# Who loads wk and who loads wv: swapping two weight loads between SyncE's and ScalarE's queues at the start of an attention and MLP kernel

## The chip, the cores and the metric

The kernel runs on one core of one Trainium2 chip. The metric is the device time of one execution in microseconds (us), taken as the median of several runs. The changed kernel is timed beside the kernel before on the same chip.

## What is computed

The reference mixes two branches of the same x (2048 tokens of 512 features, bf16) by a gate of one number per token. Branch A is attention with 32 heads of 16 features in four segments of 512 tokens: causal softmax attention inside a segment, plus a read of a memory M, z that earlier segments have filled. Branch B is a gated MLP of width 1792.

```python
q, k, v = x @ wq, x @ wk, x @ wv              # split into 32 heads, 4 segments
for s in range(4):
    p = softmax(qs @ ks.T * scale + mask)
    a_dot = p @ vs
    a_mem = (phi(qs) @ M) / (phi(qs) @ z + 1e-6)
    o = sigmoid(beta) * a_mem + (1 - sigmoid(beta)) * a_dot
    M, z = M + phi(ks).T @ vs, z + phi(ks).sum()
a = concat(o) @ wo
b = (relu(x @ W_gate) * (x @ W_up)) @ W_down
g = sigmoid((x * gate_w).sum(-1))
out = g * a + (1 - g) * b
```

## The kernel before

The program is recorded as a list of operations with what they read and write, and a planner in the file (class Sched) then writes one instruction stream for each engine. It places operations by priority queues with assumed durations and landing times of loads, and inserts the semaphore waits. LAND0 (L36) holds such assumed landing times for the first loads. They change no instruction by themselves; they can only change the order that the planner writes, and which of 16 DMA semaphores a load gets. Once the order is written, each engine runs its own in that order.

The work goes by segments of 512 tokens. For each, TensorE does the projections of Q and K (L797, for the first segment's Q L802) and of V (L795), the attention products (L924, L980), the MLP's two input products (L1054) and its output product (L1093). ScalarE does the exponentials, VectorE most copies out of PSUM, GpSimd the causal masks, and SyncE (SP) issues nearly all DMAs.

The change is in the start, where nothing is in SBUF yet. All matmuls of the projections need x with the features on the partitions, xT (four tiles of 128 features by 512 tokens). For the first segment it comes in two ways:

- Tokens 0 to 255 are loaded as they lie (into hT, L628, from SP). TensorE transposes them with eight matmuls against an identity (L710), two for each of the four feature tiles, into four PSUM banks. Four copies (L717) bring them to xT. The list at L701 says which engine does each copy: VectorE, ScalarE, VectorE, VectorE.
- Tokens 256 to 383 and 384 to 511 come by two transposing DMAs from SP (L632, ldxb2 and ldxb3), straight into xT.

The loop at L629 issues the weights. Each of wq, wk and wv is four loads of 128 KB, one for each 128 input features. wq goes to SP (its last quarter to ScalarE's queue), wk to ScalarE's queue, wv to SP. The two transposing DMAs are put in SP's list just ahead of wv. SP then issues the halves of W_gate and W_up, and small tensors.

ScalarE's queue is a list of its own: lact holds three tiny loads, the quarter of wq and the warming of the exponential's table, then comes its copy of xT, and behind it the four loads taken out as `wks` (L651, L721):

```python
    wks = lact[1:5]
    lact = [lact[5], lact[0]] + lact[6:] + [tab]
    ...
    sc.queue(0, lact + xcs["act"] + wks)
```

TensorE's order in the first segment (L830 to L833) is: warming matmuls, the eight transposes, Q for tokens 0 to 255 (sixteen matmuls, feature tile by feature tile, the four column blocks in turn), Q for tokens 256 to 383 (sixteen), Q for 384 to 511 (sixteen), the first two column blocks of K (feature tile by feature tile, two matmuls for each, so that each quarter of wk is waited for in turn), the other two of K, and then V, which takes wv's four quarters. Attention and MLP follow.

Of the kernel before, what the change touches and what calls it, by code (L numbers as in the profile page):

```python
# [32 lines left out]
H1_T = 14000.0  # L33
LX = 300.0
DCOST = {"ldwg0_0": 1000.0, "ldbraw": 1800.0, "ldgwb": 1300.0, "ldx1_0": 1500.0, "vsh0": 1100.0, "vsh1": 1100.0, "vsh2": 1100.0, "vsh3": 1100.0}
LAND0 = {"ldhT0": 2850.0, "ldxb2": 3700.0, "ldxb3": 3500.0, "ldwq0": 2950.0, "ldwq1": 3050.0, "ldwq2": 3100.0, "ldwq3": 3700.0, "ldwk0": 2800.0, "ldwk1": 2900.0, "ldwk2": 3000.0, "ldwk3": 3000.0}  # L36
NBLK = 36
QTN, EKN, HTN, OTN, XR = 8, 4, 19, 8, 3
SBX = 0
# [89 lines left out]
class Sched:  # L129
# [241 lines left out]
    def place(self, op, e, start):  # L371
# [30 lines left out]
        if op.dma:  # L402
# [7 lines left out]
            issued = start + occ  # L410
            op.end = max(self.dma_busy + self.dcost(op) if op.nbytes > 4096 and op.name not in LAND0 else 0.0, start + self.landing(op, start) + (0.0 if op.name in LAND0 else LX))
            self.dma_busy = max(self.dma_busy, op.end) if op.nbytes > 4096 else self.dma_busy
# [21 lines left out]
    def landing(self, op, start):  # L434
        kind = op.name[:2] if op.name[:3] != "ldx" or op.name[:4] == "ldxr" else "tx"
        if op.name == "ldwd":
            return 10300.0
        if op.name in LAND0:
            return LAND0[op.name]
        if kind == "ld":  # L440
# [120 lines left out]
def build_kernel(nc, A_x, A_wq, A_wk, A_wv, A_wo, A_beta, W_g, W_u, W_d, gate_w, out):  # L561
    _, S, D = A_x.shape
    F = W_g.shape[1]
    assert D == 512 and S % 512 == 0 and F % 128 == 0
    NSEG, KT, NF, NT = S // 512, D // 128, F // 128, S // 128
    EPS, SCALE = 1e-6, 16 ** -0.5
    sc = Sched(seeds=(339564, 801711, 0, 805551, 301395, 836631, 634535, 0, 524381, 836447, 792364, 880187, 245227, 322538, 537582, 772576, 302341, 920238, 2826, 48651, 0, 987459, 126639, 0, 821755, 0, 0, 0, 0, 0, 349994, 0,))
    T = {}
    with contextlib.ExitStack() as stack:
        for name, shape, dt in plan(S, D, F):  # L570
            T[name] = stack.enter_context(nc.sbuf_tensor(name, shape, dt))
        PS = stack.enter_context(nc.psum_tensor("ps", [128, 8, 512], F32))
        for st in sc.streams:
            sc.sem[st] = stack.enter_context(nc.semaphore(f"s_{st}"))
        program(sc, nc, T, PS, A_x, A_wq, A_wk, A_wv, A_wo, A_beta, W_g, W_u, W_d, gate_w, out, NSEG, KT, NF, NT, EPS, SCALE)
        with nc.Block() as block:
            sc.emit(block)
    return sc


def program(sc, nc, T, PS, A_x, A_wq, A_wk, A_wv, A_wo, A_beta, W_g, W_u, W_d, gate_w, out, NSEG, KT, NF, NT, EPS, SCALE):
    V = type("V", (), T)
# [3 lines left out]
    def op(eng, fn, occ, **k):  # L586
        return sc.add(Op([(eng, fn, occ)], **k))

    def pe(fn, occ, **k):
        k.setdefault("lat", PE_LAT)  # L590
        if k.get("role") == "w":
            k["reads"] = list(k.get("reads", ())) + [f"init{i}" for i in range(4)]
        return op("pe", fn, occ, **k)
# [13 lines left out]
    def dma(eng, fn, nbytes, occ=500.0, **k):  # L607
        return op(eng, fn, occ, dma=True, nbytes=nbytes, **k)

    def A(ep):  # L610
        return PS[:, ep.bank, :] if ep.nb == 1 else PS[:, ep.bank:ep.bank + 2, :]
# [6 lines left out]
    def load(eng, names, dst, src, nbytes, occ=474.0):  # L618
        (lact if eng == "act" else lsp).append(dma(eng, lambda e, dst=dst, src=src: e.dma_start(dst, src), nbytes, occ=occ, writes=names, name="ld" + names[0]))  # L619
# [6 lines left out]
            load_xt("sp", c, kt)  # L626
    x0 = A_x[0, 0:512, :].rearrange("(h p i) d -> h p i d", h=2, i=2)
    load("sp", ["hT0", "hT1"], V.hT[:, 0:2, :], x0[0], 1 << 18)  # L628
    for eng, nm, w, src in (("sp", "wq", V.wq, A_wq), ("act", "wk", V.wk, A_wk), ("sp", "wv", V.wv, A_wv)):  # L629
        if nm == "wv":  # L630
            for i in (2, 3):
                lsp.append(dma("sp", lambda e, i=i: e.dma_start_transpose(V.xT[:, :, 128 * i:128 * i + 128], A_x[0, 128 * i:128 * i + 128, :]), 1 << 17, occ=1250.0, writes=[f"xT0_{i + 2}"], name=f"ldxb{i}"))  # L632
        for kt in range(KT):
            load("act" if (nm, kt) == ("wq", 3) else eng, [f"{nm}{kt}"], w[:, kt, :], src[kt * 128:(kt + 1) * 128, :], 1 << 17)
# [58 lines left out]
    def warm(m, n, k, b):  # L693
        def fn(e):
            for i in range(m):
                ins = e.matmul(PL[:, b, 0:n], lhsT=nc.const_aps.tensor(1.0, [128, 128], BF16), rhs=nc.const_aps.tensor(1.0, [128, n], BF16), start=True, stop=True)
            return ins
        return pe(fn, m * n * (0.834 if k == 0 else 0.5), writes=[f"bankL{b}"], name=f"warm{k}")

    xps, xcs = [warm(5, 512, 0, 3), warm(6, 128, 0, 3)], {"dve": [], "act": []}  # L700
    for h, kt, bank, eng in ((0, 0, 0, "dve"), (0, 1, 1, "act"), (0, 2, 2, "dve"), (0, 3, 3, "dve")):  # L701
        ep = Epoch("att") if bank is None else None
        bk = [] if bank is None else [f"bankL{bank}"]

        def B(ep=ep, bank=bank):
            return A(ep) if bank is None else PL[:, bank, :]

        def fx(e, h=h, kt=kt, B=B):
            for i in range(2):
                ins = e.matmul(B()[:, 128 * i:128 * i + 128], lhsT=V.hT[:, 2 * h + i, kt * 128:(kt + 1) * 128], rhs=V.ident[:], start=True, stop=True)  # L710
            return ins
        xps.append(pe(fx, 205, reads=[f"hT{2 * h}", "ident"], writes=bk, name=f"xt{4 * h + kt}", ep=ep, role=ep and "w"))
        dst = V.xT[:, kt, h * 256:(h + 1) * 256].rearrange("q (t i) -> q t i", i=2)

        def cpy(e, d=dst, B=B, eng=eng):
            x = B()[:, 0:256].rearrange("q (i t) -> q t i", i=2)
            return e.tensor_copy(d, x) if eng == "dve" else e.activation(d, x, ACT.Copy)  # L717
        xcs[eng].append(op(eng, cpy, 430 if eng == "dve" else 390, reads=bk, writes=[f"xT0_{kt + 4 * h}"], name=f"xc{4 * h + kt}", ep=ep, role=ep and "r"))
# [495 lines left out]
```

## Time and profile before

| | |
|---|---|
| time, median of 3 runs | 264.72 us (264.42 to 264.75) |
| the profiled execution, its own time | 264.86 us |
| its span in the profile | 263.1 us |
| TensorE (PE) busy | 254.3 us, 97% of the span |
| VectorE (DVE), ScalarE (ACT), GpSimd (POOL) busy | 182.4, 181.1, 128.6 us |
| DMA queue of the loads issued by SP (q1) | 18.80 MB, 30.9% of 16 engines over the span |
| DMA queue of the loads issued by ScalarE (q10) | 0.66 MB, 1.2% |

The profile is of one execution. A row of its timeline gives start and duration in us, the engine (PE matmuls, PEld weight loads of TensorE, SPq and ACTq the DMA-issuing instructions of SP and ScalarE), the line of the kernel, and what is written from what; x4 stands for four instructions in a row. The duration of a DMA-issuing instruction is only the issuing; "DMA to landing" is from the start of the issue to the data's being there. In brackets stands how long the engine was idle before, and what released it. The time outside the span, 264.86 less 263.1, is 1.76 us.

### The profile page before, as it was taken

Reading aid. Unit: us, or ns where it says so; the run is one execution under the profiler, and the core shown is the slowest. Engines: PE = TensorE matmul, PEld = TensorE weight load, DVE = VectorE, ACT = ScalarE, POOL = GpSimd, SP = SyncE. Lnnn points to the kernel's source line nnn. Section 1 sums busy time; section 2 is a strip of 40 time slices with the busy share of each in tenths; the row PEclk is TensorE's granted clock in tenths of the full one; section 3 lists DMA queues with packets and bytes.
Section 4 is the critical chain, followed back from the end, with each engine's and each line's share of the span. In section 5 each row is a group of like instructions: output and inputs, shape, how many; then the busy total and the mean of one; then the engine's idle time right before and its main releaser. Section 6 shows DMA issues by size and latency. Waiting matters only on the chain.

```text
span 263.1 us, 6472 instructions
## 1 busy us (share of the span) xinstructions
PE 254.3 (97%) x2643; PEld 114.9 (44%) x2677; DVE 182.4 (69%) x359; ACT 181.1 (69%) x153; POOL 128.6 (49%) x295
## 2 busy tenths in 40 slices
PE   8799999999999999999999999999999999999996
PEld 4533444443434544344344544444444434344444
DVE  4489888887787586887888588757575627478600
ACT  2377689879889678796777688677777566756021
POOL 3016533576558356665746386646364344444100
PEclk9999999999999999999999999999999999999999
DMA  7999653392515143202040430000031500000011
GB/s 176 314 349 207 152 51 41 90 342 54 82 40 108 27 79 80 75 8 43 22 107 20 62 102 2 22 4 20 13 81 36 59 21 22 22 0 2 0 42 40
DMA packets 35869, 19.87 MB, mean 76 GB/s; under 512 B 25088, under 2 KB 35200, under 8 KB 35840
## 3 DMA queue, kind: packets, MB, share of 16 engines
q1 hardware_dynamic: 35024, 18.80, 30.9%
q10 hardware_dynamic: 816, 0.66, 1.2%
q8 instruction: 21, 0.34, 0.5%
q14 instruction: 8, 0.07, 0.1%
HBM read 10.14 MB, written 2.11 MB: 47 GB/s over the span
## 4 chain that ended last, share of the span: by engine, by line
PE 92%; DVE 2%; DMA 2%; issue 2%; SPq 1%; POOL 0%
PE ps L1054 37%; PE ps L1093 18%; PE ps L924 9%; PE ps L797 8%; PE ps L980 7%; PE ps L1086 5%; PE ps L795 5%; DMA xT<-in_A_x_dram 2%; PE ps L867 1%; PE ps L847 1%; SPq L619 1%; SPq L632 0%; PE ps L802 0%; POOL E L946 0%; DVE kp L820 0%
## 5 line engine op out<-in xcount | busy, mean ns | idle before, releaser
L946 POOL TENSOR_SCALAR_AFFINE_SELECT E<-E 64x256 bf16<-64x256 bf16 (+1 forms) x256 | 108.8, 435 | 112.7 <-ACT E L940 84.5
L940 ACT ACTIVATE E<-ps 128x2048 bf16<-128x2048 f32 x72 | 135.0, 1876 | 40.9 <-PE ps L924 40.4
L1054 PE MATMUL ps<-xT,wg 128*128 128x512 bf16 x217 | 58.6, 380 | 0.8 <-issue 0.5
L1054 PE MATMUL ps<-xT,wu 128*128 128x512 bf16 x216 | 57.8, 380 | 1.0 <-issue 0.8
L1093 PE MATMUL ps<-wd,hT 128*128 128x512 bf16 (+2 forms) x227 | 52.1, 366 | 1.5 <-issue 1.4
L1065 DVE TENSOR_TENSOR hT<-ps,rl 128x512 bf16<-128x512 f32 x56 | 38.2, 683 | 14.4 <-PE ps L1054 13.0
L1054 PEld LDWEIGHTS ps<-xT,wu 128*128 128x128 bf16 x224 | 20.6, 98 | 25.6 <-issue 2.6
L1093 PEld LDWEIGHTS ps<-wd,hT 128*128 128x128 bf16 x238 | 21.2, 98 | 23.6 <-issue 2.6
L990 DVE STREAM_TRANSPOSE Tn<-ps 128x512 f32<-128x512 f32 x32 | 21.2, 695 | 14.6 <-PE ps L980 14.6
L1054 PEld LDWEIGHTS ps<-xT,wg 128*128 128x128 bf16 x224 | 19.9, 98 | 25.6 <-issue 4.7
L1063 DVE TENSOR_SCALAR rl<-ps 128x512 bf16<-128x512 f32 x35 | 24.1, 687 | 8.5 <-PE ps L1054 8.2
L924 PE MATMUL ps<-qT,kp 32*128 32x192 bf16 (+7 forms) x512 | 28.6, 287 | 0.0
L924 PEld LDWEIGHTS ps<-qT,kp 32*128 32x128 bf16 x512 | 8.2, 92 | 26.2 <-issue 11.4
L980 PE MATMUL ps<-E,vaug 64*17 64x128 bf16 (+7 forms) x512 | 18.7, 283 | 0.0
L980 PE MATMUL ps<-E,vsh 64*17 64x128 bf16 (+7 forms) x512 | 18.3, 283 | 0.0
L1103 ACT ACTIVATE osb<-ps,omg 128x512 bf16<-128x512 f32 (+1 forms) x9 | 6.1, 675 | 17.7 <-PE ps L1086 14.0
L1062 ACT ACTIVATE rl<-ps 128x512 bf16<-128x512 f32 x21 | 12.5, 596 | 7.2 <-PE ps L1054 7.1
L1086 PE MATMUL ps<-wo,oT 128*128 128x512 bf16 (+2 forms) x66 | 16.0, 366 | 0.1
L797 PE MATMUL ps<-xT,wk 128*128 128x512 bf16 x62 | 15.8, 379 | 0.2 <-issue 0.2
L1102 DVE TENSOR_SCALAR osb<-ps,omg 128x512 bf16<-128x512 f32 (+1 forms) x8 | 5.3, 665 | 15.2 <-PE ps L1086 10.4
L795 PE MATMUL ps<-wv,xT 128*128 128x512 bf16 x62 | 15.4, 380 | 0.2 <-issue 0.2
L980 PEld LDWEIGHTS ps<-E,vaug 64*17 64x17 bf16 x512 | 11.6, 86 | 8.3 <-issue 3.0
(70 smaller groups left out, 232.7 us busy)
## 6 DMA issues: line engine op xcount, KB each, us to landing
vsh<-vaug SPq DMA_DIRECT2D x8, 272.0 KB, 3.6
osb<-in_A_x_dram SPq DMA_DIRECT2D x16, 128.0 KB, 2.3
out_dram<-osb SPq DMA_DIRECT2D x15, 128.0 KB, 1.7
wg<-in_B_W_gate_dram SPq DMA_DIRECT2D x8, 224.0 KB, 5.4
wu<-in_B_W_up_dram SPq DMA_DIRECT2D x8, 224.0 KB, 6.4
wd<-in_B_W_down_dram SPq DMA_DIRECT2D x1, 1792.0 KB, 8.7
wk<-in_A_wk_dram ACTq DMA_DIRECT2D x4, 128.0 KB, 4.3
wv<-in_A_wv_dram SPq DMA_DIRECT2D x4, 128.0 KB, 4.2
```

Source lines behind the costliest of these rows:

```text
L795: ins = e.matmul(A(ep)[:, :], lhsT=V.xT[:, kt, tok + col * 128:tok + (col + 1) * 128], rhs=w[:, kt, :], start=(kt == 0), stop=(kt == KT - 1))
L797: ins = e.matmul(A(ep)[:, :], lhsT=w[:, kt, col * 128:(col + 1) * 128], rhs=V.xT[:, kt, tok:tok + 512], start=(kt == 0), stop=(kt == KT - 1))
L924: ins = q.matmul(dst, lhsT=V.kp[r, kslot(s, G), c, :], rhs=V.qT[r, qslot(s, G), q0:q0 + w], start=True, stop=True, tile_position=(32 * jj, ...
L940: acts.append(act(lambda a: a.activation(V.E[:, base * 512:base * 512 + min(2048, 4 * W)], PF[:, 0:min(2048, 4 * W)], ACT.Exp, scale=SCALE ...
L946: pools.append(pool(lambda g, ap=ap, lim=lim, pat=pat: g.affine_select(out=ap, in_=ap, compare_op=ALU.is_ge, fill=0.0, base=lim, pattern=[ ...
L980: ins = q.matmul(A(eps[p])[32 * jj:32 * jj + 17, 64 * (c + u):64 * (c + u + n)], lhsT=v[:, 8 * G + 2 * jj + p, :], rhs=V.E[r, f:f + 64 * n ...
L990: ds.append(dve(lambda e, p=p, ep=eps[p]: e.transpose(V.Tn[:, 2 * (G % (TNN // 2)) + p, :], A(ep)[:, :]), t_dve(512), writes=[f"Tn{2 * (G ...
L1054: ins = e.matmul(A(ep)[:, :], lhsT=w[:, kt, f * 128:(f + 1) * 128], rhs=V.xT[:, kt, c % XR * 512:(c % XR + 1) * 512], start=(kt == 0), sto ...
L1063: ("dve", lambda e, ep=eg, r=r: e.tensor_scalar(V.rl[:, r, :], A(ep)[:, :], 0.0, None, ALU.max), t_dve(512))],
L1065: evs.append(dve(lambda e, ep=eu, r=r, hs=hs: e.tensor_tensor(V.hT[:, hs, :], A(ep)[:, :], V.rl[:, r, :], ALU.mult), t_dve(512), reads=[f" ...
L1086: ins = e.matmul(A(ep)[:, 0:c1 - c0], lhsT=V.oT[:, ot[G], i * 128:(i + 1) * 128], rhs=V.wo[:, G, c0:c1], start=st_ and G == 0, stop=sp_ an ...
L1093: ins = e.matmul(A(ep)[:, 0:c1 - c0], lhsT=V.hT[:, slots[f], i * 128:(i + 1) * 128], rhs=V.wd[:, f, c0:c1], start=st_ and f == f0, stop=sp ...
```

## The change

wk's four loads go to SP, behind the second transposing DMA, where wv's stood. wv's four loads go to ScalarE's queue, where wk's stood (the list `wks` now holds wv's). The fourth copy of xT (feature tile 3) goes from VectorE to ScalarE, so that ScalarE's queue has two copies ahead of those loads. The planner's assumed landing times of wk become 2850 for each quarter. In the order that the planner writes, each engine's other instructions stand as before; some of the loads use another of the 16 DMA semaphores.

```diff
-LAND0 = {..., "ldwk0": 2800.0, "ldwk1": 2900.0, "ldwk2": 3000.0, "ldwk3": 3000.0}
+LAND0 = {..., "ldwk0": 2850.0, "ldwk1": 2850.0, "ldwk2": 2850.0, "ldwk3": 2850.0}
...
-    for eng, nm, w, src in (("sp", "wq", V.wq, A_wq), ("act", "wk", V.wk, A_wk), ("sp", "wv", V.wv, A_wv)):
-        if nm == "wv":
+    for eng, nm, w, src in (("sp", "wq", V.wq, A_wq), ("sp", "wk", V.wk, A_wk), ("act", "wv", V.wv, A_wv)):
+        if nm == "wk":
             for i in (2, 3):
                 lsp.append(dma("sp", lambda e, i=i: e.dma_start_transpose(...), ..., name=f"ldxb{i}"))
         for kt in range(KT):
             load("act" if (nm, kt) == ("wq", 3) else eng, [f"{nm}{kt}"], w[:, kt, :], src[kt * 128:(kt + 1) * 128, :], 1 << 17)
...
-    for h, kt, bank, eng in ((0, 0, 0, "dve"), (0, 1, 1, "act"), (0, 2, 2, "dve"), (0, 3, 3, "dve")):
+    for h, kt, bank, eng in ((0, 0, 0, "dve"), (0, 1, 1, "act"), (0, 2, 2, "dve"), (0, 3, 3, "act")):
```

More of the change, by code (lines that the diff above doesn't have):

```diff
@@ L35 @@
 DCOST = {"ldwg0_0": 1000.0, "ldbraw": 1800.0, "ldgwb": 1300.0, "ldx1_0": 1500.0, "vsh0": 1100.0, "vsh1": 1100.0, "vsh2": 1100.0, "vsh3": 1100.0}
-LAND0 = {"ldhT0": 2850.0, "ldxb2": 3700.0, "ldxb3": 3500.0, "ldwq0": 2950.0, "ldwq1": 3050.0, "ldwq2": 3100.0, "ldwq3": 3700.0, "ldwk0": 2800.0, "ldwk1": 2900.0, "ldwk2": 3000.0, "ldwk3": 3000.0}
+LAND0 = {"ldhT0": 2850.0, "ldxb2": 3700.0, "ldxb3": 3500.0, "ldwq0": 2950.0, "ldwq1": 3050.0, "ldwq2": 3100.0, "ldwq3": 3700.0, "ldwk0": 2850.0, "ldwk1": 2850.0, "ldwk2": 2850.0, "ldwk3": 2850.0}
 NBLK = 36
```

## The prediction

> **What bounds the kernel now.** I read the page first, then the waits of TensorE, then the chain of work that ended last, cut to the first 30 us, because the change touches only instructions that run before 10 us.
>
> ```profile
> span 263.1 us, 6472 instructions
> PE 254.3 (97%) x2643; PEld 114.9 (44%) x2677; DVE 182.4 (69%) x359; ACT 181.1 (69%) x153; POOL 128.6 (49%) x295
> ...
> PE ps L802 <- DMA xT<-in_A_x_dram: 1.3, 1, 1.3
> ...
> 4.02 4.87 DMA xT<-in_A_x_dram
> 8.88 0.05 issue
> 8.93 1.07 PE ps L802 x16
> 10.00 0.05 issue
> 10.05 3.40 PE ps L797 x15
> ```
>
> The first two rows say that TensorE is busy for 97% of the span, so what moves its first matmuls moves the end, nearly one for one. The waits (total, times, longest) show one DMA wait on TensorE in the whole run: 1.3 us of the Q projection (L802) for x. The chain says which: the second transposing DMA of x, in flight from 4.02 to 8.88 us. Sixteen matmuls of Q follow it, then the K projection (L797) from 10.05. All that the change can do to the time it does by moving the 8.88, or by making K wait where it doesn't wait today. 1.3 us, 0.5% of the span, is the largest gain from the first.
>
> **The change, part by part.** These are the rows of the timeline at the place (start, duration, engine and line), and below them the time from issue to landing of the four wk loads and the two transposing loads, and of the first and the last wv load alone.
>
> ```profile
> 3.65 0.63 PE L710 MATMUL ps<-ident,hT 128*128 128x128 bf16 x8
> 3.98 1.09 DVE L717 CAST xT<-ps 128x256 bf16<-128x256 f32 x3 [0.83 <-PE ps L710]
> 4.09 0.38 ACT L717 ACTIVATE xT<-ps 128x256 bf16<-128x256 f32 x1
> 4.10 1.95 ACTq L619 DMA_DIRECT2D wk<-in_A_wk_dram  x4
> 4.46 3.16 PE L802 MATMUL ps<-xT,wq 128*128 128x256 bf16 x32 [0.18 <-DVE xT L717]
> 5.32 2.00 SPq L619 DMA_DIRECT2D wv<-in_A_wv_dram  x4
> 9.87 1.09 ACT L808 ACTIVATE qT<-ps 128x512 bf16<-128x512 f32 x2 [5.39 <-DMA wk<-in_A_wk_dram]
> 11.17 0.43 SPq L619 DMA_DIRECT2D gwb<-in_gate_w_dram  x1
> 13.29 1.89 PE L795 MATMUL ps<-wv,xT 128*128 128x512 bf16 x8
> ...
> DMA to landing us min/median/max: 3.5/4.3/4.5
> DMA to landing us min/median/max: 3.5/4.2/4.9
> L619 SPq DMA_DIRECT2D wv<-in_A_wv_dram x1: 582/582/582, 5.3 to 5.3; - x1
> DMA to landing us min/median/max: 4.4/4.4/4.4
> L619 SPq DMA_DIRECT2D wv<-in_A_wv_dram x1: 430/430/430, 6.9 to 6.9; - x1
> DMA to landing us min/median/max: 4.1/4.1/4.1
> ```
>
> The copy first. VectorE loses one of three copies (1.09/3 = 0.36 us) and ScalarE gains one of 0.38. TensorE's transposes end at 3.65 + 0.63 = 4.28, so the second copy starts when the first ends, 4.09 + 0.38 = 4.47, and ends at 4.85, before VectorE's third did (3.98 + 1.09 = 5.07). TensorE needs it for the last quarter of the first Q matmuls. They end at 4.46 + 3.16 = 7.62, 1.3 us ahead of the x it then waits for. So the copy is worth nothing in itself; without that cover it would be 0.2 us, 5.07 less 4.85. ScalarE has nothing else to do until 9.87.
>
> What the copy does is delay the loads behind it. Today the first wk load is issued at 4.10, just after the copy starts. Behind a second copy I put wv's first issue at 4.4 to 4.5 and its last end near 6.4. That wv is late harms nobody: with the 4.5 us of the slowest wk load, the last piece lands before 11 and is first used at 13.29.
>
> Now wk on SP. It takes the four places of wv, so SP issues as much as before and nothing behind it moves, but for its waits: each load waits for the semaphore it reuses, and gwb, at 11.17, now follows the first wk load, which lands by about 9.7. At wv's durations wk lands at 5.3 + 4.4 = 9.7 to 6.9 + 4.1 = 11.0. K's first eight matmuls go through wk's four pieces, two matmuls each; by the chain's 3.40 us for 16 (one record is missing) a pair takes 0.43, so the pieces are wanted at 10.05, 10.48, 10.90 and 11.33. The margins are 0.35 and 0.33 at the two ends: wk is in time today, but no longer by much, and TensorE can't come forward by more than about 0.3 unless wk does.
>
> So two terms are left: when the second transposing DMA lands, and whether wk, now behind it in the same queue, slips. The shares of the two queues (q1 is SP's, q10 is ScalarE's: packets, MB, share of 16 engines), in five windows, 4.4 to 5.1, 5.1 to 5.7, 5.7 to 6.3, 6.3 to 7.5 and 7.9 to 9.3 us:
>
> ```profile
> q1 hardware_dynamic: 471, 0.16, 102.1%
> ...
> q10 hardware_dynamic: 84, 0.08, 56.8%
> q1 hardware_dynamic: 145, 0.03, 30.2%
> ...
> q1 hardware_dynamic: 332, 0.08, 90.7%
> q10 hardware_dynamic: 45, 0.03, 57.3%
> ...
> q10 hardware_dynamic: 102, 0.10, 72.2%
> q1 hardware_dynamic: 154, 0.04, 20.3%
> ...
> DMA packets 521, 0.45 MB, mean 318 GB/s; under 512 B 86, under 2 KB 521, under 8 KB 521
> ```
>
> First window: SP's queue alone, the first transposing load goes through. Second: a gap in SP's queue, in which ScalarE's takes 0.08 MB of wk. Third: the second transposing load starts, briskly. Fourth: wk's packets hold 72% of the engines for 0.10 MB in 1.2 us, and the tail of the transposing load creeps. The landings say the same: 3.5 us for the first, 4.9 for the second. That tail is the 1.3 us that TensorE waits.
>
> After the change wv stands where wk stood, 0.3 to 0.4 us later. The same competitor is there in the fourth window. What moved in the gap (84 packets) can now stand beside the transposing load instead of ahead of it: 0.08 MB at the 318 GB/s of the last window is 0.25 us. So the landing moves by between -1.4 (as quick as the first, 3.5 for 4.9) and about +0.3 (all of the lost gap); I take +0.1, nearest to the second, since the competitor stays. For wk: behind the transposing load it shared the engines with two leftover ACT loads today and shares with about three afterwards, the same 0.25 us at most on the last pieces, against a margin of 0.33. I take +0.1 for what of it shows on TensorE. Everything behind is in the same order on each engine, and no DMA wait of TensorE follows that could swallow or add to it.
>
> The Trainium skill's page "DMA: Bandwidth & Descriptors", section "Issuing engines are not separate DMA queues", says that loads from several engines run on the same DMA engines and interleave, so that spreading them saves only issue time. By that rule alone the swap of engines would be worth 0, and the sum 264.7; the trace agrees in so far as both queues share the engines in the windows above.
>
> The sum: 0 for the copy, +0.1 for the landing, +0.1 for wk, so +0.2. The profiled execution took 264.86 us (span 263.1 and 1.76 around it), and 265.06 is what it would become; the median of the runs, 264.72, is 0.14 lower, and becomes 264.9.
>
> **The rivals.** *The transposing load escapes (faster).* The later start of the ACT loads takes them out of its tail, and it lands in 3.5 us as the first did, at 7.5. Q would end 1.3 earlier; but wk then has to come through with all of wv beside it. Eight loads of 0.13 MB are 1.05 MB. Today the second to fourth windows have moved 0.21 MB of them on ScalarE's queue by 7.5 us, some 0.25 by 7.9, when the transposing load is off the engines, and the other 0.8 at 318 GB/s take 2.5 us, to 10.4; the last piece lands at 11.0, 0.6 later. With the transposing load off at 6.6 and 0.1 MB moved by then, 0.95 MB take 3.0 us, to 9.6, and wk's last piece lands at 10.2 against 11.33 wanted today: a gain of 1.1. Half an escape gives 0.4 to 0.5. For it: the first transposing load, alone, took 3.5, and the third window shows the second one brisk too. Against: ACT's loads run into the same window, all four. Time: 263.6 to 264.3, 263.9 as its middle.
>
> *wk comes too late (slower).* The place is K's first eight matmuls; the mechanism is that wk, needed first, is queued behind the transposing load and shares the engines with wv, which is needed 3 us later. It decides once wk's last piece takes over 4.5 us to land (11.33 less 6.9), and costs over 0.2% once it takes 5.0. Loads issued further back in SP's queue show how far that can go:
>
> ```profile
> L619 SPq DMA_DIRECT2D wu<-in_B_W_up_dram x2: 430/431/432, 10.2 to 10.7; - x2
> DMA to landing us min/median/max: 5.1/5.8/6.6
> ```
>
> With 5.1 to 5.8 the last piece lands at 12.0 to 12.7: +0.7 to +1.3, less if only the first is delayed. For it: no margin over 0.35, and every slip of the transposing load now carries wk along. Against: the first and the last of the same places gave wv 4.4 and 4.1. Time 265.2 to 266.0, its middle 265.6. The same page, section "Queues, rings and completion order", has each DMA engine take turns between the queues that have work; by that rule wk gets every second turn while wv has packets left, which speaks for this case, and no row here tells the turns apart.
>
> *The change doesn't delay the ACT loads.* If ScalarE issues its loads while the second copy is still waiting for the engine, wv starts within 0.1 us of wk's old time. The transposing load lands as today and wk in wv's old times: 264.7.
>
> **How the numbers follow.** Forecast case 0.42, the escape 0.26, late wk 0.28, no delay 0.04. 0.2% is 0.53 us, about what a measurement of this kernel can tell from no change: under 264.19 is faster, over 265.25 slower. The forecast case has its own range, 264.4 to 265.4, and gives 0.34 to the same, 0.07 to slower, 0.01 to faster. The escape gives 0.24 to faster and 0.02 to the same, late wk 0.28 to slower, no delay 0.04 to the same. Faster 0.25, same 0.40, slower 0.35. The range runs from 263.8, inside the escape, to 265.9, inside late wk, and leaves out a little of both ends.
>
> **What would show it.** In the profile after: TensorE's wait for the transposing load between 1.2 and 1.6 us, its landing 4.8 to 5.2 us after issue; wv's first issue on ScalarE at 4.4 to 4.5; wk's landings at 4.1 to 4.6 us; no wait of L797 for wk over 0.2. A transposing load under 4.5 us with K starting before 9.7 would be the escape; a wait of L797 for wk over 0.5 the late wk. A difference that arises after 20 us would make the whole account wrong.

## The result, and the profile after

The changed kernel takes 265.19 us (median of 21 runs, 264.59 to 265.99), the kernel before beside it 264.58 us (21 runs, 264.17 to 265.37). The ratio is 1.0023, 95% interval 1.0016 to 1.0030: slower by 0.6 us. That is just past the 0.53 us (0.2%) that had been named as the bound, with an interval that reaches to both sides of it, and inside the range.

First the waits of TensorE and the chain at the start, of the kernel after (the same views as before; waits in total, times, longest):

```profile
span 263.5 us, 6472 instructions
...
PE ps L797 <- DMA wk<-in_A_wk_dram: 0.8, 2, 0.6
PE ps L802 <- DMA xT<-in_A_x_dram: 0.6, 2, 0.3
...
5.94 4.59 DMA wk<-in_A_wk_dram
10.53 0.05 issue
10.58 3.19 PE ps L797 x14
```

Q's wait for x has fallen from 1.3 us to 0.6, and a wait that wasn't there before has come: K for wk, 0.8. The chain no longer goes through the second transposing load but through the second piece of wk, issued at 5.94 and landed at 10.53.

Then the timeline of the kernel after at the same place, and the time from issue to landing of the two transposing loads and of wk's four loads:

```profile
4.07 0.76 DVE L717 CAST xT<-ps 128x256 bf16<-128x256 f32 x2 [0.91 <-PE ps L710]
4.22 0.38 ACT L717 ACTIVATE xT<-ps 128x256 bf16<-128x256 f32 x1
4.46 0.35 ACTq L619 DMA_DIRECT2D wv<-in_A_wv_dram  x1
4.51 0.38 ACT L717 ACTIVATE xT<-ps 128x256 bf16<-128x256 f32 x1
8.35 1.07 PE L802 MATMUL ps<-xT,wq 128*128 128x128 bf16 x16 [0.35 <-DMA xT<-in_A_x_dram]
10.04 0.38 PE L797 MATMUL ps<-xT,wk 128*128 128x512 bf16 x1 [0.62 <-DMA wk<-in_A_wk_dram]
13.61 1.89 PE L795 MATMUL ps<-wv,xT 128*128 128x512 bf16 x8
...
DMA to landing us min/median/max: 4.2/4.3/4.3
DMA to landing us min/median/max: 4.4/4.5/4.6
```

The second transposing load lands after 4.3 us instead of 4.9, the first after 4.2 instead of 3.5; wk on SP takes 4.4 to 4.6, where wv had taken 4.1 to 4.4 in the same places. V starts at 13.61 instead of 13.29. That 0.32 is the difference of the two profiled executions: 265.19 less 264.86 is 0.33.

How far does one profile speak for all? Both kernels were profiled twice more.

> The kernel before, profiled once more, to see how far one profile speaks for all. If landings repeat: the second transposing load 4.7 to 5.0 us after issue, wk on ScalarE's queue 3.5 to 4.5, K from 10.0 to 10.2 without a wait for wk. If they scatter: the landing anywhere from 4.3 to 5.0, K's start with it.

> The changed kernel, profiled once more. If landings repeat: the second transposing load 4.2 to 4.4 us after issue, wk 4.4 to 4.6, waits of K for wk of 0.6 to 0.9 in sum, V from 13.5 to 13.8. If they scatter: the two trade places from run to run, and V starts anywhere from 13.3 to 14.3.

> A third profile of the kernel before. If the time is the start of V plus a constant (251.4 us in the profiles so far), V starts at the time of this run less 251.4, between 12.9 and 13.6, without a wait of K for wk over 0.3.

> A third profile of the changed kernel. V starts at its time less 251.4, between 13.2 and 14.2; by theory A a later V goes with waits of K for wk, not with a later transposing load.

The landings scatter. V's first row in the three profiles of before (the first of them is in the prediction), then in the other two of after:

```profile
13.11 1.89 PE L795 MATMUL ps<-wv,xT 128*128 128x512 bf16 x8
12.94 1.89 PE L795 MATMUL ps<-wv,xT 128*128 128x512 bf16 x8
13.08 1.89 PE L795 MATMUL ps<-wv,xT 128*128 128x512 bf16 x8
13.38 1.89 PE L795 MATMUL ps<-wv,xT 128*128 128x512 bf16 x8
```

| profiled execution | its time | V starts | difference |
|---|---|---|---|
| before | 264.86 | 13.29 | 251.57 |
| before, second | 264.71 | 13.11 | 251.60 |
| before, third | 264.52 | 12.94 | 251.58 |
| after | 265.19 | 13.61 | 251.58 |
| after, second | 264.65 | 13.08 | 251.57 |
| after, third | 264.95 | 13.38 | 251.57 |

The time is V's start plus 251.6, to 0.03 us, in both kernels. (The expectations say 251.4; they counted from where the chain enters V, 0.2 later.) So in these executions all of the change, and all of the scatter from run to run, lies ahead of V. What no three profiles give is the mean: they were at 264.7 and 264.9, while the medians of 21 runs are 0.6 apart. For sizes I go by the timed runs, for mechanisms by the rows.

The third profile of after shows the mechanism at its plainest (waits, timeline, then the landings of the two transposing loads and of wk):

```profile
PE ps L797 <- DMA wk<-in_A_wk_dram: 1.3, 1, 1.3
...
5.80 2.75 PE L802 MATMUL ps<-xT,wq 128*128 128x256 bf16 x38
9.89 3.65 PE L797 MATMUL ps<-xT,wk 128*128 128x512 bf16 x15 [1.34 <-DMA wk<-in_A_wk_dram]
...
DMA to landing us min/median/max: 3.4/3.5/3.5
DMA to landing us min/median/max: 4.2/4.3/4.3
```

Here the transposing loads took 3.4 and 3.5 us, Q ran through without waiting for x and was done at 8.55, and the whole of what was won was lost again to wk.

### The profile page after: what moved, and what is told of

Read it like the earlier page. It is cut to its first block, busy times and chain, and to the rows that moved or that the text cites. A ratio compares the mean times of both kernels' runs of the same rounds, so it can differ in the third digit from the quotient of the medians.

```text
span 263.5 us, 6472 instructions
## 1 busy us (share of the span) xinstructions
PE 254.7 (97%) x2643; PEld 114.8 (44%) x2677; DVE 182.2 (69%) x358; ACT 181.5 (69%) x154; POOL 128.8 (49%) x295
## 4 chain that ended last, share of the span: by engine, by line
PE 91%; DVE 2%; issue 2%; SPq 2%; DMA 2%; POOL 0%
PE ps L1054 37%; PE ps L1093 18%; PE ps L924 9%; PE ps L797 8%; PE ps L980 7%; PE ps L1086 5%; PE ps L795 5%; DMA wk<-in_A_wk_dram 2%; PE ps L867 1%; SPq L632 1%; SPq L619 1%; PE ps L847 1%; POOL E L946 0%; DVE kp L820 0%; DVE vaug L829 0%
## 5 line engine op out<-in xcount | busy, mean ns | idle before, releaser
L797 PE MATMUL ps<-xT,wk 128*128 128x512 bf16 x62 | 16.0, 379 | 0.9 <-DMA wk<-in_A_wk_dram 0.8
L1102 DVE TENSOR_SCALAR osb<-ps,omg 128x512 bf16<-128x512 f32 (+1 forms) x8 | 5.3, 665 | 15.2 <-PE ps L1086 10.4
```

Of the source, the lines that this page charges most:

```text
L797: ins = e.matmul(A(ep)[:, :], lhsT=w[:, kt, col * 128:(col + 1) * 128], rhs=V.xT[:, kt, tok:tok + 512], start=(kt == 0), stop=(kt == KT - 1))
```

## The experiments

Theory A: two effects of opposite sign. ACT's loads, started later, let the second transposing load land earlier; and wk, behind it on SP and beside wv, is late by more than that. Rivals: the copy does nothing, the transposing load lands earlier because wv stands where wk stood, and wk alone costs the time (B); wk is late because of its place in SP's queue, whatever runs beside it (C); the bytes up to W_up bound the start in any order (D); the cost lies elsewhere (E).

### Which part of the change costs

The copy alone, on the kernel before:

```diff
-    ... (0, 3, 3, "dve")):
+    ... (0, 3, 3, "act")):
```

> The kernel before with only the fourth copy of xT moved to ScalarE; wk stays on ScalarE's queue, now 0.36 us later, wv on SP. Theory A (two effects: later ACT loads let the second transposing load land 0.5 us earlier, and wk behind it on SP is late): TensorE's wait for x falls from 1.3 to about 0.7 us, wk on ScalarE lands before it is wanted, K starts near 9.5 instead of 10.05, time 0.4 to 0.6 us below before. Theory B (the copy does nothing, the earlier landing came from wv standing where wk stood): landing 4.9 us as before, time within 0.2 us of before.

Measured: ratio 0.9996 (0.9988 to 1.0005), 264.65 against 264.62. The second transposing load landed after 4.5 us in its profile, as in the third of before without the edit, so the profile doesn't single out the copy. The gain that A wanted, 0.4 to 0.6, didn't come; B's "within 0.2" holds.

The loads alone, with the copy back on VectorE:

> The changed kernel with the fourth copy back on VectorE: only the loads are swapped. Theory A: the second transposing load is held by ACT loads at the old time again and lands 4.9 us after issue, wk behind it on SP: its last pieces 0.2 to 0.4 us late, K's first eight matmuls end 0.3 to 0.6 us later than before, time 0.3 to 0.6 us above before. Theory B: as the changed kernel, landing at 4.3, time +0.3 to +0.6 by wk alone.

Measured: 1.0022 (1.0013 to 1.0031), 265.17 against 264.62, the same as the whole change. So the swap of the loads is the cost, and the copy is worth nothing. Its profile (264.84) is the quickest of its runs, with a transposing load of 3.9 us, where A wanted 4.9, and a wait of K for wk of 0.6: A has the sign of wk right and this landing wrong. B has the time of both kernels right.

The later start of ScalarE's loads, which A made the reason for the earlier landing, doesn't go with it. With wk on ScalarE's queue the second transposing load took 4.9, 4.7 and 4.5 us (before), 4.5 (the copy alone) and 4.4 (before with K from wq, below). With wv there it took 4.3, 4.4 and 3.4 (after), 3.9 (the loads alone) and 3.5 (after with K from wq). But in the loads alone ScalarE's first load was issued at 4.24, as in before (4.10 to 4.25), and in the copy alone at 4.67, as late as in two profiles of after. So, as far as one profile each of these two can tell, the earlier landing goes with the swap of the loads and not with the delay; why wv there holds it up less than wk did stays open.

### What the wait for wk is worth

K of the first segment is multiplied with wq, and the four waits for wk's loads move to V (here and in the next edits, a comment stands in place of the lines that move the instructions):

```diff
-            ep = pj(V.wk, G, "k", "wk")
+            ep = pj(V.wq if s == 0 else V.wk, G, "k", "wk")
...
     sc.run()
+    # the four waits on wk's loads move to the first matmul of V
```

> The changed kernel, in which K of the first segment is multiplied with wq instead of wk, so that K waits for no wk load; all loads are issued as in the changed kernel, and V waits for wk instead, which has landed by then. K of that segment is thus not the reference's. Theory A (the swap costs because wk is late): the 0.6 us come back and more, since the transposing load lands no later than before: 0.0 to 0.5 us below before. Theory E (the swap costs by the transposing load or elsewhere): time stays 0.4 to 0.7 us above before.

> The same in the kernel before: K of the first segment is multiplied with wq and waits for no wk load (and isn't the reference's). wk lands ahead of its use there, so both theories: within 0.2 us of before. A gain of 0.3 us or more would say that before often waits for wk too, in runs that its profiles don't show.

Measured: on the changed kernel 263.85 against 264.61, ratio 0.9965 (0.9947 to 0.9984); on the kernel before 264.25, ratio 0.9983 (0.9964 to 1.0003). The first, in its timeline:

```profile
5.82 2.78 PE L802 MATMUL ps<-xT,wq 128*128 128x256 bf16 x37
8.65 3.40 PE L797 MATMUL ps<-xT,wq 128*128 128x512 bf16 x15
11.88 1.89 PE L795 MATMUL ps<-wv,xT 128*128 128x512 bf16 x8
```

No wait from 5.82 on, V at 11.88, and the time of that execution 263.46, which is 251.58 later. E falls: without K's wait for wk the changed kernel goes from 0.61 above before to 0.76 below (each against the kernel before timed beside it), so the wait costs about 1.4 us, more than A had put down (0.6 to 1.1). Two single profiles say the same: with the second transposing load landing after 3.5 us here and 3.4 in the third profile of after, V starts at 11.88 without the wait and at 13.38 with it. On the kernel before the same edit gives 0.36, with an interval that holds no change; whether before waits for wk in some runs stays open. Between the two without that wait the swap is a gain of 0.4 us, but the intervals overlap, so its size isn't settled.

### What makes wk late

wv on SP too, behind wk, so that no load of ScalarE's queue runs beside the transposing loads or wk:

```diff
     sc.run()
+    # wv's four loads: from ScalarE's list to SP's, behind the last of wk
```

> The changed kernel with wv's four loads on SP too, behind wk; the order written by the planner stays otherwise. No ACT load runs beside the transposing loads or wk. Theory A (sharing with the ACT loads is what holds both): the second transposing load lands 3.5 to 3.7 us after issue, wk 2.3 to 3.3, K starts at 8.7 to 9.0 without a wait for wk over 0.2, wv lands near 10.5, time 1.0 to 1.4 us below before. Theory C (wk is late because of its place in SP's queue behind the transposing load, whatever else runs): wk still takes 4.2 to 4.6 us, K waits for wk by 0.6 to 1.5, time at or above before.

And wv still on ScalarE, but issued only when the second transposing load has landed:

```diff
     sc.run()
+    # ahead of wv's first load, ScalarE waits for the semaphore of ldxb3
```

> The changed kernel with one wait more: ScalarE issues wv only when the second transposing load has landed. Theory A: transposing load and wk as in the kernel with all on SP, K from 8.7 to 9.0; wv issued at 7.6 to 9.5 beside the loads of W_gate lands at 11.5 to 13 and may cost V up to 0.7 us; time 0.5 to 1.3 us below before. Theory C: wk takes 4.2 to 4.6 us, time at or above before.

All on SP: ratio 1.0012 (1.0001 to 1.0023), 264.82. The rows of its profile are the two transposing loads, wk, the start of K and of V, and what is late next, the waits for W_up; last, W_up's landings here and in the kernel before:

```profile
DMA to landing us min/median/max: 2.8/3.1/3.4
DMA to landing us min/median/max: 2.2/2.4/2.6
8.82 3.62 PE L797 MATMUL ps<-xT,wk 128*128 128x512 bf16 x16
12.27 1.91 PE L795 MATMUL ps<-wv,xT 128*128 128x512 bf16 x8
PE ps L1054 <- DMA wu<-in_B_W_up_dram: 1.8, 2, 1.4
...
DMA to landing us min/median/max: 7.2/7.3/7.5
DMA to landing us min/median/max: 4.7/4.9/6.6
```

C falls: in the same places of the same queue wk lands in 2.2 to 2.6 us instead of 3.7 to 4.6 in the three profiles of after, and the second transposing load in 2.8 instead of 3.4 to 4.4, once wv isn't beside them. K starts at 8.82 and V at 12.27. But the time didn't follow (A wanted 1.0 to 1.4 below before): V's 1.0 us are given back, and more, to W_up, which SP issues four places later and which then takes 7.3 us to land. (This profile, 266.04, is the slowest of its 12 runs, 264.31 to 266.04; in the median less was given back.) One queue didn't keep the DMA engines busy either. The windows 7.9 to 10.2 us, all on SP and then before, DMA share and GB/s last:

```profile
7.90:10.20 2.30, 2.30 (x27) 1.59 (x25) 1.29 (x2) 1.09 (x2) 0.00 (x0) 1.00 0.85 267
...
7.90:10.20 2.30, 1.22 (x17) 1.10 (x19) 0.28 (x1) 0.33 (x1) 0.00 (x0) 1.00 1.11 332
```

SP issues a load of 128 KB every 0.47 us (wk's third at 6.39, its fourth at 6.87), by estimate 280 GB/s at most, which is about what the first row shows. That the issuing is the limit there is argued from these two numbers and not tested.

In before and after, all eight loads of wk and wv together are done at about the same time: the last lands 11.0 to 11.1 us into the three profiles of before and 10.9 to 11.3 into those of after. The swap only decides whose it is. In before it is wv's, and wk's last piece lands at 10.0 to 10.4; in after it is wk's.

With the wait before wv: 1.0016 (1.0004 to 1.0027), 265.02, where A wanted 0.5 to 1.3 below before. Its transposing load lands in 2.6 us and wk in 2.2 to 3.4, K's wait is 0.4; then V waits for the last piece of wv, which took 5.4 us beside W_gate:

```profile
PE ps L795 <- DMA wv<-in_A_wv_dram: 0.4, 1, 0.4
PE ps L797 <- DMA wk<-in_A_wk_dram: 0.4, 1, 0.4
...
13.52 1.47 PE L795 MATMUL ps<-wv,xT 128*128 128x512 bf16 x6 [0.45 <-DMA wv<-in_A_wv_dram]
```

### Trying for a version that beats both

wv on SP behind wk, and four loads of the MLP's weights on ScalarE's queue after the second transposing load, W_gate's first half or W_up's:

```diff
     sc.run()
+    # wv: to SP behind wk; ldwg0_* (or ldwu0_*): to ScalarE, behind a wait for ldxb3
```

> The changed kernel with wv on SP behind wk, and the first half of W_gate (four loads) on ScalarE's queue instead, issued when the second transposing load has landed; SP is ahead by two microseconds again for W_up. Theory A (start bound by what shares the DMA engines with the load that is next needed, then by W_up's landing): transposing load lands 2.6 to 3.0 us after issue, wk in 2.2 to 3.4, K starts near 8.8, wv by 12, first W_up matmul near 17.6 with a wait under 0.5; time 0.6 to 1.2 us below before. Theory D (the sum of bytes up to W_up's first half bounds the start, whatever the order): the first W_up matmuls wait as with all on SP, time within 0.4 us of before.

> As the kernel before it in this call, with W_up's first half on ScalarE's queue instead of W_gate's. Theory A: as that one, but W_up is now issued ahead of W_gate and lands before it, W_gate's first pieces (first used near 16.2) land by 16; time 0.6 to 1.2 us below before. Theory D: the wait moves to W_gate, time within 0.4 us of before.

Measured: 1.0045 (1.0032 to 1.0058) with W_gate, 1.0039 (1.0025 to 1.0052) with W_up. Both theories missed: neither W_up nor W_gate was late, wk was, again, and more than in any other kernel. The two kernels' rows for K:

```profile
11.74 2.33 PE L797 MATMUL ps<-xT,wk 128*128 128x512 bf16 x10 [1.47 <-DMA wk<-in_A_wk_dram]
...
10.52 0.60 PE L797 MATMUL ps<-xT,wk 128*128 128x512 bf16 x2 [1.31 <-DMA wk<-in_A_wk_dram]
11.39 2.33 PE L797 MATMUL ps<-xT,wk 128*128 128x512 bf16 x10 [0.27 <-DMA wk<-in_A_wk_dram]
```

With W_up, wk's last two pieces took 4.1 and 4.5 us, about as long as beside wv, though W_up's loads (224 KB instead of 128) were issued only after 6.8. With W_gate, issued after 6.7, K's last ten matmuls had to wait until 11.74, 4.9 us after the last piece of wk was issued. (The landings of wk listed for that run, 2.4 to 3.1 us, are those of the other three pieces; the last one's is not complete in the trace.) K was ready early in both, at 8.8 and 8.2, so the waits are long. That fits A's mechanism: in every order that was run, something needed soon came late, beside or behind something needed later. Of the orders of loads, none beats the kernel before. D isn't settled: no order was found that brings all of it in time, which isn't a proof that none exists.

## Why the prediction was right or wrong

**The number: inside the range, in part by luck.** The forecast was +0.2, from two small costs. What came was +0.6, from a gain of about 0.8 and a cost of about 1.4, neither of them in the sum at that size.

**What bounds the start: right.** All of the difference lies ahead of V, and TensorE passes it to the end one for one, to 0.03 us in the six profiles.

**The copy, nothing: right**, 0.9996 alone. ScalarE's first wv load was issued at 4.46 in the first profile of after, as put (4.4 to 4.5), and at 4.67 in the other two.

**The landing of the second transposing load, +0.1: wrong in sign.** It landed after 4.3 and 4.4 us and in the third profile 3.4, against 4.9, 4.7 and 4.5 before. The step that failed is that the lost gap (0.08 MB) would move beside the transposing load and hold it longer. It went sooner instead, as the escape rival had it, but not by that rival's reason either: the experiments on the copy and on the loads tie the earlier landing to the swap and not to the later start, and its cause stays open. With K from wq in both kernels the swap is 0.4 us quicker, which isn't settled.

**wk, +0.1: right in mechanism, mis-sized.** The term rested on a margin of 0.33 us and a shift of 0.25. The shift was about right: wk's last piece landed at 10.9 to 11.3, where wv's in the same place had landed at 11.0 to 11.1. The margin was wrong, for two reasons. It was counted from K's start at 10.05, but the row at 10.05 has only 15 of K's 16 matmuls, and the missing one is the first: K's weight loads start at 9.78 in that profile. So K began near 9.8, and the margin of wk was about 0.1 us. The third profile of before has the same gap, 16 weight loads from 9.4 and 15 matmuls from 9.7:

```profile
L797 PEld LDWEIGHTS ps<-xT,wk x16: 98/98/98, 9.4 to 12.5; 128*128 128x128 bf16 x16
L797 PE MATMUL ps<-xT,wk x15: 379/379/379, 9.7 to 12.7; 128*128 128x512 bf16 x15
```

And as soon as x lands earlier, K wants wk earlier too, at 8.6 when nothing holds Q (the third profile: Q done at 8.55, K's row only from 9.89). The wait is worth 1.4 us in the timed runs, where the term was 0.1 and the rival of late wk gave up to 1.3. So both rivals were there in the same kernel: an escape worth about 0.8, between its half (0.4 to 0.5) and its whole (1.1), and late wk that takes it and 0.6 more. The likeliest class, the same within 0.53 us, was just missed by the medians. Of the signs, the transposing load's landing (4.8 to 5.2) and TensorE's wait for it (1.2 to 1.6) came in none of the three profiles, and "no wait of L797 over 0.2" was wrong in two of them, where the waits were 0.8 and 1.3.

**The rules weighed there.** By the Trainium skill's page "DMA: Bandwidth & Descriptors", section "Issuing engines are not separate DMA queues", the swap would be worth 0; it measured +0.6. The rule holds as far as sharing goes (wk and wv do share), but it doesn't say which of two loads is needed first, and that is what the swap changed. What it leaves to the queues, issue time, may have become a bound when everything was on SP (267 GB/s for 332). The Trainium skill's other rule, in "Queues, rings and completion order" of the same page, turns between the queues, fits wk's 4.5 us beside wv for 2.4 alone; no row here shows single turns.

**The scatter was not foreseen.** The first profile of before, with 4.9 us, was its slowest of three; the 1.3 us of wait on which the sum began were 0.4 in the second, and in the third no such wait was listed.

## What to carry to other kernels

At a start where loads for several steps share the DMA engines, ask of each load not how long it takes but what runs beside it and which of the two is needed first: the same load in the same queue took 2.4 or 4.5 us here. A margin counted against today's timeline is gone once the wait ahead of it is mended, so follow each gain to the load that is late next. Count the matmuls of a row before taking its start for the start of the work: here the first one's record was missing and made a margin of 0.1 us look like 0.3. Where landings scatter by half a microsecond, take three profiles before building a sum on one wait, and find the point (here V's start) from which on all executions are alike.

## What the runs showed of the hardware that was not expected

A transposing DMA and the plain loads behind it react strongly to plain loads on another queue: the second transposing load took 3.4 to 4.9 us from issue to landing beside 128 KB loads from ScalarE's queue (ten profiles), and 2.6 to 2.8 in the four kernels in which ScalarE issued no such load before it had landed; wk on SP took 2.2 to 2.6 with wv on SP too, against 3.7 to 4.6 beside wv on ScalarE's queue. And the time to landing is not the same in every execution of one program: the second transposing load took 4.9, 4.7 and 4.5 us in the kernel before and 4.3, 4.4 and 3.4 in the one after, with TensorE's clock granted in full (1.0).
